# Scaled weight tables from PSUM, earlier weight loads, and a prologue divided otherwise between three engines

## Chip, cores and metric

One core of a Trainium2 chip. The metric is the device time of one execution in microseconds; a kernel is given by the median of several executions. Besides the time there is a traced execution of each kernel, whose span is about 1.8 us shorter than its time.

## The reference

```python
X = np.fft.fft(x, axis=1)               # x: 8 x 3008 x 256
X = np.fft.fft(X, axis=2).real          # mixing along sequence and model dimension
t = X.reshape(24064, 256)
out = (np.maximum(t @ w_gate, 0) * (t @ w_val)) @ w_out     # 256 -> 1536 -> 256
```

The kernel folds the second transform into the weights. `wc` and `ws` are cosine and sine transforms of `w_gate` and `w_val`, and `wm = s2 * ws` serves the mirrored half of the spectrum. The first transform is made in pieces of 94 x 32 points, with tables that the prologue makes from iotas and sines.

Of the kernel before, what the change touches and what calls it, by code (L numbers as in the profile page):

```python
# [11 lines left out]
F32 = mybir.dt.float32  # L12
BF16 = mybir.dt.bfloat16
I32 = mybir.dt.int32
ALU = mybir.AluOpType
ACTF = mybir.ActivationFunctionType
SB = bass.MemoryType.SB
PS = bass.MemoryType.PSUM
RND = 12582912.0
WARM = 15  # L20
FIRST = 15


# [21 lines left out]
def kernel(ctx: ExitStack, tc, x, w_gate, w_val, w_out, out):  # L45
# [3 lines left out]
    nc = tc.nc  # L49
    B, S, D = x.shape  # L50
    DF = w_gate.shape[1]
    NA, NB = 94, 32
# [100 lines left out]
    t1t = {}  # L153
# [27 lines left out]
    psf, tabs = {}, {}  # L181

    def ends(r, n):

        v = xt[0]["lo" if r < NB // 2 else "hi"][0:NA, r % 16:r % 16 + n, :]
        if r < NB // 2:
            nc.vector.tensor_copy(tabs["back"][:, r:r + n, 0:1], v[:, :, H:H + 1])
        else:
            nc.vector.tensor_copy(tabs["back"][:, r:r + n, 0:1], v[:, :, 0:1])
            nc.vector.tensor_copy(v[:, :, 0:1], v[:, :, H:H + 1])  # L190

    def back(r, n, evac):

        dst = tabs["back"][:, r:r + n, 1:H]
        src = free(xt[0]["lo" if r < NB // 2 else "hi"][0:NA], r % 16 * D + D - 1, [D, n], [-1, H - 1])
        if evac == "act":
            nc.scalar.copy(dst, src)
        else:
            nc.vector.tensor_copy(dst, src)
# [23 lines left out]
    def first_evac(c, evac):  # L223

        if 0 not in t1t:
            t1t[0] = tp.tile([128, 16, D], BF16, tag="t1", bufs=1, name="t1")
        dst = free(t1t[0][:], 2 * c, [1536, 2], [16, 96], [1, 2])
        src = free(psf[c], 0, [96, 2], [1, 96], [192, 2])
        plain = nc.scalar.copy if evac == "act" else nc.vector.tensor_copy
        plain(dst, src)  # L230
        if c == 0:
            plain(free(t1t[0][0:1], 1536, [16, 96]), psf[0][0:1, 384:480])
# [54 lines left out]
    w1 = const.tile([NA, 16, 96], BF16, tag="w1")  # L287
    wz = const.tile([NA, 3, 2, 96], BF16, tag="wz")
# [28 lines left out]
    def pair_w(n, i, eng, parts=(0, 1)):  # L317

        lo, hi, up = (wst[i, n, c] for c in range(3))
        if 0 in parts:  # L320
            eng.tensor_tensor(up, lo, hi, op=ALU.add)
        if 1 in parts:
            eng.tensor_tensor(lo, lo, hi, op=ALU.subtract)

    def fold_w(n, i, cs, ps=None):

        ps = ps or spare("psw")
        for k, w in ((0, wst[i, n, 2]), (1, wst[i, n, 0])):
            nc.tensor.matmul(ps[64 * k:64 * k + 64, :], lhsT=cd[:, cs, 64 * k:64 * k + 64], rhs=w,  # L329
                             start=True, stop=True)  # L330
        nc.scalar.copy((wc, ws)[cs][i][:, n * 512:(n + 1) * 512], ps[:])

    def scale_w(n, i):

        sl_ = slice(n * 512, (n + 1) * 512)
        nc.vector.tensor_scalar(wm[i][:, sl_], ws[i][:, sl_], scalar1=s2[:], scalar2=None, op0=ALU.mult)  # L336

    def nyquist():

# [6 lines left out]
    with tc.tile_pool(name="sp", bufs=1, space=SB) as sp:  # L346
        dve, pl = nc.vector, nc.gpsimd
# [14 lines left out]
        def absolute(out, a):  # L362
            nc.scalar.activation(out, a, ACTF.Abs)

        def iota(eng, out, pattern, base, mult):
            eng.iota(out, pattern=pattern, base=base, channel_multiplier=mult, allow_small_or_imprecise_dtypes=True)
# [26 lines left out]
        def warm(n):  # L393

            for k in range(n):
                nc.tensor.matmul(psk[:], lhsT=wk[:, 512:640], rhs=wk[:, 0:512], start=True, stop=True)
# [19 lines left out]
        iota(pl, kbi[:, 0, :], [[1, NB]], NB // 2, 0)  # L416
        iota(pl, kbi[:, 1:4, :], [[0, 3], [1, NB]], 0, 0)
        load_w(0, pl)
        iota(pl, di[:], [[-32, 4], [-16, 2], [-1, 16]], 0, 1)
        pl.memset(ro[:], 0.0)  # L420
        pl.tensor_scalar(s2[:], mi[:], scalar1=1.0, scalar2=-2.0, op0=ALU.min, op1=ALU.mult)

        def angles(lo, hi):
            t, q = tt[:, lo:hi, :], tq[:, lo:hi, :]
# [6 lines left out]
            cosines(free(wn[:], 1536 + 96 * a, [96, b_ - a], [2, 48]), tq[:, a:b_, :], S)  # L431
            sines(free(wn[:], 1536 + 96 * a + 1, [96, b_ - a], [2, 48]), tt[:, a:b_, :], S, -1.0)

        def negate(a, b_):
            dve.tensor_scalar(wn[:, 0, a:b_, :], wn[:, 1, a:b_, :], scalar1=-1.0, scalar2=None, op0=ALU.mult)  # L435

        def bits(shift, mask):
            ti = sp.tile([128, 1], I32, tag=f"b{shift}{mask}i")
            dve.tensor_scalar(ti[:], pi[:], scalar1=shift, scalar2=mask,
                              op0=ALU.logical_shift_right, op1=ALU.bitwise_and)  # L440
            tf = sp.tile([128, 1], F32, tag=f"b{shift}{mask}f")
            dve.tensor_copy(tf[:], ti[:])
            return tf

        def col(tag, a, *args, **kw):
            t = sp.tile([128, 1], F32, tag=tag)
            dve.tensor_scalar(t[:], a[:], *args, **kw)
            return t

        def group(cs, upper):  # L450
            for k in (0, 1):
                for c in cs:
                    first_products(c, upper, k)
# [3 lines left out]
        angles(9, J)  # L457
        dve.memset(wz[:], 0.0)
        table(9, 16)
        negate(1, 9)  # L460
        ends(0, 8)
        back(2, 6, "dve")
        group((1, 2, 3), False)
        warm(9)
        jj, sl, up, odd = bits(0, 15), bits(4, 1), bits(5, 3), bits(0, 1)
        z = col("z", jj, scalar1=0.0, scalar2=None, op0=ALU.is_equal)
        negate(9, 16)
        back(0, 2, "dve")
        both = (free(tt[:], 0, [16 * 48, 2], [1, 48]), free(tq[:], 0, [16 * 48, 2], [1, 48]))
        cosines(free(wz[:], 0, [97, 2], [2, 48]), both[1], S)  # L470
        for k in range(2):
            sines(free(wz[:], 192 * (k + 1), [97, 2], [2, 48]), both[0], S, 2.0 * k - 1.0)
        dve.tensor_scalar(tabs["wzn"][:], wz[:, 0], scalar1=-1.0, scalar2=None, op0=ALU.mult)
        nz = col("nz", z, scalar1=-1.0, scalar2=1.0, op0=ALU.mult, op1=ALU.add)
        mul = col("mul", z, scalar1=sl[:], scalar2=16.0, op0=ALU.mult, op1=ALU.mult)
        mul = col("mul2", mul, scalar1=jj[:], scalar2=None, op0=ALU.add)
        o0 = col("o0", nz, scalar1=sl[:], scalar2=-8.0, op0=ALU.mult, op1=ALU.mult)
        o0 = col("o1", o0, scalar1=8.0, scalar2=None, op0=ALU.add)
        o1 = col("o2", nz, scalar1=8.0, scalar2=o0[:], op0=ALU.mult, op1=ALU.add)
        nc.scalar.copy(w1[:, 1:16, :], wn[:, 1, 1:16, :])  # L480
        ends(24, 8)
        back(25, 3, "act")
        back(28, 3, "dve")
        back(24, 1, "act")
        back(31, 1, "dve")
        group((1, 2, 3), True)
        warm(2)
        ends(8, 4)
        dve.tensor_scalar(dd[:], dd[:], scalar1=mi[:], scalar2=None, op0=ALU.mult)
        residue(dd[:], dq[:], D, dve)  # L490
        back(8, 4, "act")
        first_evac(1, "dve")
        absolute(dq[:], dd[:])
        first_evac(2, "act")
        first_evac(3, "dve")
        cosines(cd[:, 0, 1:H], dq[:, 1:H], D)
        sines(cd[:, 1, 1:H], dd[:, 1:H], D, 1.0)
        dve.tensor_copy(cd[:, 1, 0:1], odd[:])
        dve.tensor_scalar(cd[:, 0, 0:1], odd[:], scalar1=-1.0, scalar2=1.0, op0=ALU.mult, op1=ALU.add)

        sv, ti = [], []

        def turns(cs):
            ti.append(sp.tile([128, 4, NB], I32, tag=f"m2i{cs}", name="ti"))
            sv.append(sp.tile([128, 4, NB], F32, tag=f"m2s{cs}", name="sv"))
            dve.tensor_scalar(ti[cs][:], kbi[:], scalar1=mul[:], scalar2=(o0, o1)[cs][:], op0=ALU.mult, op1=ALU.add)
            dve.tensor_scalar(ti[cs][:], ti[cs][:], scalar1=NB - 1, scalar2=None, op0=ALU.bitwise_and)
            nc.scalar.activation(sv[cs][:], ti[cs][:], ACTF.Sin, scale=2.0 * math.pi / NB * (1.0 - 2e-7), bias=npi[:])

        group((4, 5), False)  # L510
        warm(4)
        ends(20, 4)
        back(20, 4, "dve")
        group((4, 5), True)
        warm(2)
        ends(12, 4)
        ends(16, 4)
        back(12, 4, "act")
        back(16, 4, "act")
        turns(0)  # L520
        turns(1)
        dve.tensor_scalar(ui[:], ui[:], scalar1=up[:], scalar2=-1.0, op0=ALU.is_equal, op1=ALU.mult)
        first_evac(4, "act")
        first_evac(5, "dve")
        for cs in range(2):
            dve.tensor_tensor(m2[:, cs, :].rearrange("p (u k) -> p u k", u=4), sv[cs][:], ui[:], op=ALU.mult)
        group((6, 7, 0), False)
        warm(1)
        group((6, 7, 0), True)
        pair_w(0, 0, dve)  # L530
        first_evac(6, "act")
        nc.sync.dma_start(out=seen[:], in_=t1t[0][0:1, 0, 12:14])
        load_w(1, nc.sync)
        load_w(2, nc.sync)
        load_x(1, 0, nc.sync, False)
        first_evac(7, "dve")
        first_evac(0, "act")

        pl.tensor_scalar(ro[:, :, 0, 1:16], di[:, :, 0, 1:16], scalar1=16.0, scalar2=-1.0,
                         op0=ALU.is_equal, op1=ALU.mult)  # L540
        pl.tensor_scalar(ro[:, :, 1, 1:16], di[:, :, 1, 1:16], scalar1=-16.0, scalar2=None, op0=ALU.is_equal)
# [14 lines left out]
        stage2(0, 0, 0, "act")  # L556
        fold_w(0, 1, 0, g_tile())
        stage2(0, 0, 1, "dve")
        scale_w(0, 0)
        fold_w(0, 1, 1)  # L560
        scale_w(0, 1)

        pair_w(1, 0, pl)
        load_x(1, 0, None)
# [181 lines left out]
    def at(t, fn, *args):  # L746
        extra.setdefault(t, []).append(lambda: fn(*args))

    for n in (1, 2):
        for k, t in enumerate(((1, 2, 2, 3), (4, 5, 6, 7))[n - 1]):  # L750
            at(t, fold_w, n, k // 2, k % 2)
            if k % 2:
                at(t, scale_w, n, k // 2)
    for t, blk, cs, e in ((1, 1, 1, "dve"), (3, 1, 0, "dve"), (4, 2, 1, "dve"), (6, 2, 0, "dve")):
        at(t, upright, blk, cs, e)
    at(3, rotate, 0, 4, 8)
# [109 lines left out]
```

## The kernel before: what the change touches

Weights come in six 512-column parts (n = 0 to 2, i = 0 for gate, 1 for value). GpSimd or DVE make sums and differences (`pair_w`), TensorE folds them, ACT evacuates, and DVE scales the sine table, here from SBUF:

```python
    def fold_w(n, i, cs, ps=None):
        ps = ps or spare("psw")          # spare: one of two PSUM banks, by turns
        ...                              # two matmuls
        nc.scalar.copy((wc, ws)[cs][i][:, n * 512:(n + 1) * 512], ps[:])

    def scale_w(n, i):
        sl_ = slice(n * 512, (n + 1) * 512)
        nc.vector.tensor_scalar(wm[i][:, sl_], ws[i][:, sl_], scalar1=s2[:], scalar2=None, op0=ALU.mult)
```

Near the end of the prologue (cut):

```python
        group((4, 5), True)              # first products 4 and 5, upper half
        warm(2)                          # warm-up matmuls
        ...
        turns(0); turns(1)               # index (DVE), mask (DVE), sine (ACT)
        ...
        first_evac(4, "act")             # behind the two sines on ACT
        first_evac(5, "dve")
        ...
        group((6, 7, 0), False); warm(1); group((6, 7, 0), True)
        pair_w(0, 0, dve)
        first_evac(6, "act")
        nc.sync.dma_start(out=seen[:], in_=t1t[0][0:1, 0, 12:14])   # holds SP until evacuation 6
        load_w(1, nc.sync); load_w(2, nc.sync); load_x(1, 0, nc.sync, False)
        first_evac(7, "dve"); first_evac(0, "act")
```

Behind it comes a ramp of twelve steps into which the other folds are mixed; `rotate` is one small matmul with a small evacuation (a copy out of PSUM), and takes its bank (one PSUM buffer) from the same two as the folds. In the profiles `psw` are the products of the folds, `ps` the first products and stage 2's, `psr` that of a rotation; `G` and `V` are the gate and value products of a step, `h` their elementwise product, `po` the output products, and a product is called mirrored when its table is `wm`:

```python
    for n in (1, 2):
        for k, t in enumerate(((1, 2, 2, 3), (4, 5, 6, 7))[n - 1]):
            at(t, fold_w, n, k // 2, k % 2)
            if k % 2:
                at(t, scale_w, n, k // 2)
    ...
    at(3, rotate, 0, 4, 8)
    at(6, rotate, 0, 8, NKA)
```

## Time and profile before

| | kernel before |
|---|---|
| time, median of 3 | 629.81 us (629.6 to 630.03) |
| span traced | 628.5 us (an execution of 630.34 us) |
| first product of the weight tables (`psw`) | 18.68 us |
| first output product (`po`) | 55.25 us |
| 289th output product (the first of the second batch) | 130.38 us |

I read every trace by these marks, in us from the start of the span. Up to the first `psw` lies the prologue; from there to the first `po` the ramp; up to the 289th `po` the end of the first batch and the entry of the second. (The recorded expectations count the products from 0 and call the 289th the 288th.) What a kernel gains is read between marks, not from the busy shares.

The other view is the list of TensorE's waits (engine, line, tile, releaser: us in total, times, longest), between 20 and 56 us:

```profile
PE V L638 <- DVE h L651: 1.5, 3, 0.7
PE psr L259 <- ACT wc L331: 0.4, 1, 0.4
PE psr L259 <- ACT ws L331: 0.4, 1, 0.4
PE G L630 <- ACT gs L625: 0.2, 1, 0.2
```

So the ramp holds 2.5 us of waits: 1.5 for products `h` (the longest, 0.7, behind the two held tables of the first step), 0.8 for two rotations (`psr`), which wait for the evacuation of the fold whose bank they take. The same view from 56 to 620 us has two lines:

```profile
PE V L638 <- DVE E L645: 0.8, 1, 0.8
PE psr L259 <- ACT gs L625: 0.2, 1, 0.2
```

Both lie between the first and the 289th output product. The scaling's mean, over all six, hides 0.35 us (at 35.06, beside no arithmetic of GpSimd's) and 1.08 (at 46.54, beside an operation of GpSimd's) (group: count, then busy us and mean ns):

```profile
L336 DVE TENSOR_SCALAR wm<-ws,s 128x512 bf16<-128x512 bf16 x6 | 5.3, 887 | 2.8 <-ACT ws L331 2.8
```

### The profile page before, as it was taken

What the parts mean: (1) busy time and instruction counts of PE and PEld (TensorE: products, weight loads), DVE (VectorE), ACT (ScalarE), POOL (GpSimd) and SP (SyncE); (2) the same over time, 40 slices, a digit from 0 to 9 for tenths busy, and PEclk for the clock granted to TensorE, in tenths of its full rate; (3) what the DMA queues carried; (4) which work ended last, traced back from release to release, by engine and by line L of the source; (5) the groups of instructions that cost most, each with busy time, mean ns of one, the idle gap of its engine ahead of it and who ended that gap; (6) DMA issues with size and microseconds to landing.
All of it is one profiled execution on the core that took longest, in us unless ns stands there. A gap on an engine that the chain in (4) does not pass through costs nothing.

```text
span 628.5 us, 11983 instructions
## 1 busy us (share of the span) xinstructions
PE 616.9 (98%) x4292; PEld 410.0 (65%) x4292; DVE 541.4 (86%) x660; ACT 444.0 (71%) x851; POOL 518.1 (82%) x445
## 2 busy tenths in 40 slices
PE   8999999999999999999999999999999999999996
PEld 4335666666666666666666666766666666666665
DVE  8677997999988998899988988899988889899991
ACT  7567777777777777777777777777687777766661
POOL 7677998998989988988989989899988866565665
PEclk9999999999999999999999999999999999999999
DMA  7697156613734263722826147441732124212114
GB/s 167 188 182 145 32 151 163 151 33 109 199 93 101 62 194 83 170 51 76 205 69 148 34 136 172 106 109 41 211 81 68 33 84 116 60 33 67 33 35 98
DMA packets 42597, 67.44 MB, mean 107 GB/s; under 512 B 5872, under 2 KB 32521, under 8 KB 40521
## 3 DMA queue, kind: packets, MB, share of 16 engines
q1 hardware_dynamic: 37944, 51.38, 32.8%
q0 software_dynamic: 4432, 15.11, 10.1%
q8 instruction: 33, 0.54, 0.4%
q14 instruction: 28, 0.22, 0.1%
q10 hardware_dynamic: 160, 0.20, 0.1%
HBM read 38.85 MB, written 30.17 MB: 110 GB/s over the span
## 4 chain that ended last, share of the span: by engine, by line
PE 94%; DVE 3%; issue 1%; ACT 1%; POOL 0%; POOLq 0%; DVEq 0%
PE po L687 40%; PE V L638 20%; PE G L630 10%; PE G L624 10%; PE G L623 9%; PE ps L162 2%; PE psw L329 2%; PE ps L271 2%; DVE h L651 1%; PE ps L216 0%; PE ps L166 0%; DVE wm L336 0%; DVE wn L435 0%; DVE E L645 0%; PE pst L240 0%
## 5 line engine op out<-in xcount | busy, mean ns | idle before, releaser
L658 POOL TENSOR_TENSOR h<-gm,E 128x992 bf16<-128x992 f32 (+1 forms) x138 | 319.9, 2318 | 83.3 <-DVE E L665 53.5
L687 PE MATMUL po<-wo,h 128*128 128x256 bf16 (+2 forms) x2304 | 328.7, 273 | 0.0
L687 PEld LDWEIGHTS <-h 128*128 128x128 bf16 (+2 forms) x2304 | 231.2, 103 | 106.0
L632 ACT ACTIVATE gm<-G 128x496 f32<-128x496 f32 (+1 forms) x288 | 170.4, 592 | 95.6 <-PE G L630 88.3
L651 DVE TENSOR_TENSOR h<-gs,V 128x1024 bf16<-128x1024 f32 (+3 forms) x150 | 173.7, 1158 | 59.8 <-PE V L638 43.2
L645 DVE SCALAR_TENSOR_TENSOR E<-nb,af,V 128x496 f32<-128x496 bf16 (+1 forms) x276 | 190.1, 730 | 1.8 <-PE G L624 1.8
L625 ACT ACTIVATE gs<-G 128x497 f32<-128x497 f32 (+2 forms) x288 | 169.6, 589 | 25.0 <-PE G L624 24.8
L665 DVE SCALAR_TENSOR_TENSOR E<-E,V 128x992 f32<-128x992 f32 (+1 forms) x138 | 164.3, 1190 | 0.0
L630 PE MATMUL G<-pq,wm 128*128 128x496 bf16 (+1 forms) x288 | 108.0, 375 | 0.3 <-ACT gs L625 0.2
L624 PE MATMUL G<-pq,ws 128*128 128x497 bf16 (+2 forms) x288 | 108.0, 375 | 0.0
L623 PE MATMUL G<-pq,wc 128*128 128x497 bf16 (+2 forms) x288 | 108.0, 375 | 0.0
L638 PE MATMUL V<-pq,ws 128*128 128x497 bf16 (+2 forms) x288 | 85.4, 375 | 0.8 <-DVE E L645 0.8
L638 PE MATMUL V<-pq,wc 128*128 128x497 bf16 (+2 forms) x288 | 85.5, 375 | 0.0
L624 PEld LDWEIGHTS <-ws 128*128 128x128 bf16 x288 | 28.2, 98 | 32.7
L700 ACT COPY os<-po 128x512 f32<-128x512 f32 x63 | 36.9, 586 | 14.7 <-PE po L687 13.8
L638 PEld LDWEIGHTS <-wc 128*128 128x128 bf16 x288 | 28.1, 98 | 20.8 <-issue 2.7
L114 POOL TENSOR_TENSOR eo<-xla 94x256 bf16<-94x256 f32 x56 | 40.3, 729 | 0.8
L623 PEld LDWEIGHTS <-wc 128*128 128x128 bf16 x288 | 28.1, 98 | 18.5 <-issue 1.2
L114 POOL TENSOR_TENSOR eo<-xlb 94x256 bf16<-94x256 f32 (+1 forms) x42 | 34.4, 820 | 0.9
L111 POOL TENSOR_TENSOR xla<-xla,xha 94x510 f32<-94x510 f32 x28 | 32.9, 1175 | 2.2
L177 ACT CAST t<-ps 96x512 bf16<-96x512 f32 x56 | 32.7, 583 | 2.4 <-PE ps L162 0.2
L630 PEld LDWEIGHTS <-wm 128*128 128x128 bf16 x288 | 28.1, 98 | 5.2 <-issue 2.6
(141 smaller groups left out, 373.9 us busy)
## 6 DMA issues: line engine op xcount, KB each, us to landing
out_dram<-os SPq DMA_DIRECT2D x124, 128.0 KB
Td<-t SPq DMA_DIRECT2D x7, 768.0 KB
t<-Td SPq DMA_DIRECT2D x7, 768.0 KB
out_dram<-os SPq DMA_DIRECT2D x82, 64.0 KB
xla<-in_x_dram SPq DMA_DIRECT2D x7, 720.0 KB
xlb<-in_x_dram SPq DMA_DIRECT2D x7, 640.0 KB
nb<-Nd SPq DMA_DIRECT2D x23, 128.0 KB
out_dram<-os SPq DMA_DIRECT2D x40, 48.0 KB
```

The costliest lines, as they stand in the source:

```text
L114: yield eng.tensor_tensor(e1[:, :, k:k + H], x1[:, :, 0:H], free(x1, D, [DX, n], [-1, H]), op=op)
L623: nc.tensor.matmul(G[:, ds], lhsT=wc[0][:, fs], rhs=pq[:, 0, ds], start=True, stop=False)
L624: nc.tensor.matmul(G[:, ds], lhsT=ws[0][:, fs], rhs=pq[:, 1, ds], start=False, stop=True)
L625: nc.scalar.activation(pair(t, "gs")[:, t % 2, ds], G[:, ds], ACTF.Relu)
L630: nc.tensor.matmul(G[:, cols], lhsT=wm[0][:, f * 128:(f + 1) * 128], rhs=pqt[b, blk][:, 1, cols], start=False, stop=True, skip_group_check ...
L632: nc.scalar.activation(pair(t, "gm")[:, t % 2, cols], G[:, cols], ACTF.Relu)
L638: nc.tensor.matmul(pair(t, "V")[:, t % 2, cs], lhsT=w[:, f * 128:(f + 1) * 128], rhs=pqt[b, blk][:, min(k, 1), cs], start=(k == 0), stop=( ...
L645: nc.vector.scalar_tensor_tensor(pair(t, "E")[:, t % 2, cols], nbt[b, blk][:, cols], af[:, f:f + 1], pair(t, "V")[:, t % 2, cols], op0=ALU ...
L651: nc.vector.tensor_tensor(pair(t, "h")[:, k, 0, 0:ds.stop - ds.start], pair(t, "gs")[:, k, ds], pair(t, "V")[:, k, ds], op=ALU.mult)
L658: eng.tensor_tensor(free(pair(t, "h")[:], 1024 * (t % 2) + 512 + w - 1, [1024, n], [-1, w]), pair(t, "gm")[:, k, cols], val[:, k, cols], o ...
L665: nc.vector.scalar_tensor_tensor(E[:, :, cols], E[:, :, cols], 2.0, V[:, :, cols], op0=ALU.mult, op1=ALU.subtract)
L687: nc.tensor.matmul(po[0:m, i, :], lhsT=pair(t - f + ff, "h")[:, ff % 2, sg, g * 128:g * 128 + m], rhs=wo[:, ff, :], start=(ff == 0), stop= ...
```

## The change

Its intent: read the scaling's input from PSUM, so that GpSimd no longer holds the scaling up (1.08 us against 0.35 in the trace of before); let W1 and W2 load earlier; release products 6, 7 and 0 earlier by evacuating product 4 ahead of the sines; and give DVE less to do in the prologue. Evacuations 5 and 7 go from DVE to ACT and evacuation 0 from ACT to DVE. The core of the diff (the other moved lines of the prologue cut):

```diff
-WARM = 15
+WARM = 12
@@ fold_w
-        nc.scalar.copy((wc, ws)[cs][i][:, n * 512:(n + 1) * 512], ps[:])
-    def scale_w(n, i):
-        nc.vector.tensor_scalar(wm[i][:, sl_], ws[i][:, sl_], scalar1=s2[:], ...)
+        nc.scalar.copy((wc, ws)[cs][i][:, sl_], ps[:])
+        if cs:
+            nc.vector.tensor_scalar(wm[i][:, sl_], ps[:], scalar1=s2[:], ...)
@@ prologue: turn indices on GpSimd, masking of both at once on DVE
+            pl.tensor_scalar(ti[cs], kbi[:], scalar1=mul[:], scalar2=(o0, o1)[cs][:], ...)
+        dve.tensor_scalar(tis[:], tis[:], scalar1=NB - 1, scalar2=None, op0=ALU.bitwise_and)
-        negate(9, 16)                                            # DVE
+        nc.scalar.mul(wn[:, 0, 9:16, :], wn[:, 1, 9:16, :], -1.0)   # ACT
@@ after the upper halves of groups (1,2,3), (4,5), and inside (6,7,0)
-        warm(2)
-        warm(2)
-        warm(1)
@@ order on ACT
-        turns(0)
-        turns(1)
         first_evac(4, "act")
-        nc.sync.dma_start(out=seen[:], in_=t1t[0][0:1, 0, 12:14])
+        nc.sync.dma_start(out=seen[:], in_=t1t[0][0:1, 0, 8:10])
         load_w(1, nc.sync)
         load_w(2, nc.sync)
         ...
+        for cs in range(2):
+            nc.scalar.activation(sv[cs][:], ti[cs], ACTF.Sin, ...)
```

More of the change, by code (lines that the diff above doesn't have):

```diff
@@ L330, in fold_w @@
                              start=True, stop=True)
-        nc.scalar.copy((wc, ws)[cs][i][:, n * 512:(n + 1) * 512], ps[:])
-    def scale_w(n, i):
         sl_ = slice(n * 512, (n + 1) * 512)
-        nc.vector.tensor_scalar(wm[i][:, sl_], ws[i][:, sl_], scalar1=s2[:], scalar2=None, op0=ALU.mult)
+        nc.scalar.copy((wc, ws)[cs][i][:, sl_], ps[:])
+        if cs:
+            nc.vector.tensor_scalar(wm[i][:, sl_], ps[:], scalar1=s2[:], scalar2=None, op0=ALU.mult)
     def nyquist():
@@ L418 @@
         load_w(0, pl)
-        iota(pl, di[:], [[-32, 4], [-16, 2], [-1, 16]], 0, 1)
-        pl.memset(ro[:], 0.0)
-        pl.tensor_scalar(s2[:], mi[:], scalar1=1.0, scalar2=-2.0, op0=ALU.min, op1=ALU.mult)
         def angles(lo, hi):
@@ L432, in table @@
             sines(free(wn[:], 1536 + 96 * a + 1, [96, b_ - a], [2, 48]), tt[:, a:b_, :], S, -1.0)
-        def negate(a, b_):
-            dve.tensor_scalar(wn[:, 0, a:b_, :], wn[:, 1, a:b_, :], scalar1=-1.0, scalar2=None, op0=ALU.mult)
         def bits(shift, mask):
@@ L459 @@
         table(9, 16)
-        negate(1, 9)
+        dve.tensor_scalar(wn[:, 0, 1:9, :], wn[:, 1, 1:9, :], scalar1=-1.0, scalar2=None, op0=ALU.mult)
         ends(0, 8)
@@ L464 @@
         warm(9)
-        jj, sl, up, odd = bits(0, 15), bits(4, 1), bits(5, 3), bits(0, 1)
-        z = col("z", jj, scalar1=0.0, scalar2=None, op0=ALU.is_equal)
-        negate(9, 16)
-        back(0, 2, "dve")
         both = (free(tt[:], 0, [16 * 48, 2], [1, 48]), free(tq[:], 0, [16 * 48, 2], [1, 48]))
@@ L472 @@
             sines(free(wz[:], 192 * (k + 1), [97, 2], [2, 48]), both[0], S, 2.0 * k - 1.0)
-        dve.tensor_scalar(tabs["wzn"][:], wz[:, 0], scalar1=-1.0, scalar2=None, op0=ALU.mult)
+        nc.scalar.mul(wn[:, 0, 9:16, :], wn[:, 1, 9:16, :], -1.0)
+        nc.scalar.copy(w1[:, 1:10, :], wn[:, 1, 1:10, :])
+        back(0, 2, "dve")
+        jj, sl, up, odd = bits(0, 15), bits(4, 1), bits(5, 3), bits(0, 1)
+        z = col("z", jj, scalar1=0.0, scalar2=None, op0=ALU.is_equal)
         nz = col("nz", z, scalar1=-1.0, scalar2=1.0, op0=ALU.mult, op1=ALU.add)
@@ L479 @@
         o1 = col("o2", nz, scalar1=8.0, scalar2=o0[:], op0=ALU.mult, op1=ALU.add)
-        nc.scalar.copy(w1[:, 1:16, :], wn[:, 1, 1:16, :])
+        dve.tensor_copy(cd[:, 1, 0:1], odd[:])
+        dve.tensor_scalar(cd[:, 0, 0:1], odd[:], scalar1=-1.0, scalar2=1.0, op0=ALU.mult, op1=ALU.add)
+        sv, ti = [], []
+        tis = sp.tile([128, 2, 4, NB], I32, tag="m2i")
+        for cs in range(2):
+            ti.append(tis[:, cs])
+            sv.append(sp.tile([128, 4, NB], F32, tag=f"m2s{cs}", name="sv"))
+            pl.tensor_scalar(ti[cs], kbi[:], scalar1=mul[:], scalar2=(o0, o1)[cs][:], op0=ALU.mult, op1=ALU.add)
+        pl.tensor_scalar(ui[:], ui[:], scalar1=up[:], scalar2=-1.0, op0=ALU.is_equal, op1=ALU.mult)
         ends(24, 8)
@@ L486 @@
         group((1, 2, 3), True)
-        warm(2)
         ends(8, 4)
+        back(8, 4, "act")
         dve.tensor_scalar(dd[:], dd[:], scalar1=mi[:], scalar2=None, op0=ALU.mult)
         residue(dd[:], dq[:], D, dve)
-        back(8, 4, "act")
+        first_evac(2, "act")
         first_evac(1, "dve")
+        first_evac(3, "dve")
+        dve.tensor_scalar(tis[:], tis[:], scalar1=NB - 1, scalar2=None, op0=ALU.bitwise_and)
         absolute(dq[:], dd[:])
-        first_evac(2, "act")
-        first_evac(3, "dve")
         cosines(cd[:, 0, 1:H], dq[:, 1:H], D)
         sines(cd[:, 1, 1:H], dd[:, 1:H], D, 1.0)
-        dve.tensor_copy(cd[:, 1, 0:1], odd[:])
-        dve.tensor_scalar(cd[:, 0, 0:1], odd[:], scalar1=-1.0, scalar2=1.0, op0=ALU.mult, op1=ALU.add)
-        sv, ti = [], []
-        def turns(cs):
-            ti.append(sp.tile([128, 4, NB], I32, tag=f"m2i{cs}", name="ti"))
-            sv.append(sp.tile([128, 4, NB], F32, tag=f"m2s{cs}", name="sv"))
-            dve.tensor_scalar(ti[cs][:], kbi[:], scalar1=mul[:], scalar2=(o0, o1)[cs][:], op0=ALU.mult, op1=ALU.add)
-            dve.tensor_scalar(ti[cs][:], ti[cs][:], scalar1=NB - 1, scalar2=None, op0=ALU.bitwise_and)
-            nc.scalar.activation(sv[cs][:], ti[cs][:], ACTF.Sin, scale=2.0 * math.pi / NB * (1.0 - 2e-7), bias=npi[:])
+        dve.tensor_scalar(tabs["wzn"][:], wz[:, 0], scalar1=-1.0, scalar2=None, op0=ALU.mult)
         group((4, 5), False)
@@ L514 @@
         group((4, 5), True)
-        warm(2)
         ends(12, 4)
+        back(12, 4, "act")
         ends(16, 4)
-        back(12, 4, "act")
-        back(16, 4, "act")
-        turns(0)
-        turns(1)
-        dve.tensor_scalar(ui[:], ui[:], scalar1=up[:], scalar2=-1.0, op0=ALU.is_equal, op1=ALU.mult)
-        first_evac(4, "act")
-        first_evac(5, "dve")
-        for cs in range(2):
-            dve.tensor_tensor(m2[:, cs, :].rearrange("p (u k) -> p u k", u=4), sv[cs][:], ui[:], op=ALU.mult)
-        group((6, 7, 0), False)
-        warm(1)
-        group((6, 7, 0), True)
-        pair_w(0, 0, dve)
-        first_evac(6, "act")
-        nc.sync.dma_start(out=seen[:], in_=t1t[0][0:1, 0, 12:14])
+        back(16, 4, "dve")
+        group((6, 7, 0), False)
+        first_evac(4, "act")
+        nc.sync.dma_start(out=seen[:], in_=t1t[0][0:1, 0, 8:10])
         load_w(1, nc.sync)
@@ L535 @@
         load_x(1, 0, nc.sync, False)
-        first_evac(7, "dve")
-        first_evac(0, "act")
+        first_evac(5, "act")
+        pair_w(0, 0, dve)
+        for cs in range(2):
+            nc.scalar.activation(sv[cs][:], ti[cs], ACTF.Sin, scale=2.0 * math.pi / NB * (1.0 - 2e-7), bias=npi[:])
+        group((6, 7, 0), True)
+        first_evac(6, "act")
+        first_evac(7, "act")
+        first_evac(0, "dve")
+        for cs in range(2):
+            dve.tensor_tensor(m2[:, cs, :].rearrange("p (u k) -> p u k", u=4), sv[cs][:], ui[:], op=ALU.mult)
+        nc.scalar.copy(w1[:, 10:16, :], wn[:, 1, 10:16, :])
+        iota(pl, di[:], [[-32, 4], [-16, 2], [-1, 16]], 0, 1)
+        pl.tensor_scalar(s2[:], mi[:], scalar1=1.0, scalar2=-2.0, op0=ALU.min, op1=ALU.mult)
         pl.tensor_scalar(ro[:, :, 0, 1:16], di[:, :, 0, 1:16], scalar1=16.0, scalar2=-1.0,
@@ L558 @@
         stage2(0, 0, 1, "dve")
-        scale_w(0, 0)
         fold_w(0, 1, 1)
-        scale_w(0, 1)
         pair_w(1, 0, pl)
@@ L751 @@
             at(t, fold_w, n, k // 2, k % 2)
-            if k % 2:
-                at(t, scale_w, n, k // 2)
     for t, blk, cs, e in ((1, 1, 1, "dve"), (3, 1, 0, "dve"), (4, 2, 1, "dve"), (6, 2, 0, "dve")):
```

## The prediction

> **What bounds the kernel now.** I read the page first (busy shares and slices), then the chain of waits in its first 60 us, then the timeline of that stretch, then, for the changed kernel, the compiled order of instructions with their semaphores.
>
> ```profile
> PE 616.9 (98%) x4292; PEld 410.0 (65%) x4292; DVE 541.4 (86%) x660; ACT 444.0 (71%) x851; POOL 518.1 (82%) x445
> PE   8999999999999999999999999999999999999996
> ```
>
> Only PE is full in every slice. By stretches it is busy 100.0 us of each 100 from 200 to 600 us, and the diff touches no line of that stretch. What the change is worth must come from the prologue (to 24 us) and the ramp (24 to 55 us, twelve steps t = 0 to 11 into which the folds of the weights are mixed). If PE enters the steady part earlier by x, the end moves by x. The chain of waits (start, us, what) shows where PE is held there:
>
> ```profile
> 14.92 0.40 ACT sv L508
> 15.32 0.40 ACT t L230
> 15.76 0.24 PE ps L216
> ...
> 23.70 1.50 DVE wm L336 x2
> 25.19 0.87 issue
> 26.06 0.67 DVE h L651
> ...
> 34.44 0.59 ACT ws L331
> 35.08 0.17 PE psr L259
> ...
> 47.54 0.66 DVE h L658
> 48.20 0.59 DVE h L651
> ```
>
> From 0.9 to 14.9 us the chain is DVE's. Between these places it is matmuls back to back. The four holds: first products 6, 7 and 0 wait for the evacuation of product 4, which stands behind two sines on ACT; the first h waits for two scaled tables; a rotation waits for the evacuation that frees its PSUM buffer; the h of step 8 waits behind a scaled table. Why these tables are slow is in the timeline:
>
> ```profile
> 23.37 1.27 POOL L321 TENSOR_TENSOR wst<-wst 128x512 f32<-128x512 f32 x1 [4.02 <-DMA wst<-in_moe_w_gate_dram]
> 23.70 2.43 DVE L336 TENSOR_SCALAR wm<-ws,s 128x512 bf16<-128x512 bf16 x2
> 24.72 1.26 POOL L323 TENSOR_TENSOR wst<-wst 128x512 f32<-128x512 f32 x1
> 35.06 0.35 DVE L336 TENSOR_SCALAR wm<-ws,s 128x512 bf16<-128x512 bf16 x1 [0.60 <-ACT ws L331]
> 46.30 1.18 POOL L111 TENSOR_TENSOR xla<-xla,xha 94x510 f32<-94x510 f32 x1
> 46.54 1.08 DVE L336 TENSOR_SCALAR wm<-ws,s 128x512 bf16<-128x512 bf16 x1 [0.73 <-ACT ws L331]
> ```
>
> Alone the scaling takes 0.35 us; beside a POOL operation it ends about 0.14 us after that one does (46.30 + 1.18 + 0.14 = 47.62, and 24.72 + 1.26 + 0.15 = 26.13).
>
> [...] I take 0.69 us from this trace's evacuation of the same shape (DVE L246 pst, 128x512, mean 688 ns). [...] the new scaling waits for ACT's semaphore, not PE's, so it still starts only after ACT's copy of the same bank. [...] Dropping warm-up matmuls leaves gaps below 1 us, so I count nothing; the trace of before shows gaps up to 0.41 us without a slowdown.
>
> **The change part by part.** Times below are on the clock of the old trace, and where they lie in the changed kernel they are estimates from its durations.
>
> (a) First products 1 to 3. Three of 15 warm-ups at 0.43 us go, but the last three were partly fast: products start at about 6.55 instead of 7.11. This gains nothing, since the upper half waits for the first high load, which ACT saw land at 9.41. On DVE, the second negation (0.68 of chain) goes to ACT, where 0.75 us lie beside idle time; the wzn table (0.13) goes later, two one-column copies (0.15) come in front. DVE is then free by about 9.2 and waits for the load; its two column moves take 0.65, so the upper half starts at 10.1, not 10.48: 0.37 gained, and two warm-ups (0.43) less before products 4 and 5.
>
> (b) The new hold. The turn indices are now made on POOL, after its four weight loads, the last of which ends at 10.70 + 1.07 = 11.77. POOL took 0.71 us for a 128x128 tensor-scalar and 0.45 to 0.50 for 128x60, so two take until about 13.2. The masking of both stands on DVE ahead of the moves of high load 20 to 23. DVE, ready at 12.45, stands still until 13.3, and then possibly until POOL's next operation lets go (13.95). With masking 0.3, wzn 0.13 and moves 0.35, products 4 and 5 upper can go at 14.1 to 14.7; before, 13.76. So most of (a) is lost.
>
> (c) Products 6, 7, 0. Product 4 is complete at about 14.7 to 15.2, ACT evacuates it at once (0.49; the sines come later), and product 0 starts at 15.25 to 15.75, not 15.76. From there to the end of the group is 18.75 - 15.76 = 2.99, less one warm-up (0.22): it ends at 18.0 to 18.5, not 18.75. Gain 0.2 to 0.7, say 0.5.
>
> (d) First step. After the group PE has fold, uprights, fold: 1.01 + 0.58 + 1.01 = 2.60. ACT copies ws (0.66 with its delay), then DVE scales wm for 0.69, and now this stands ahead of the small evacuation of the rotation (0.17). That is done 4.2 after the group, the fold of W1 part already 4.0 after: stage 2 loses 0.27. The second table: fold ends 5.6 after the group, copy 6.25, scaling 6.3 to 7.0, h 7.0 to 7.65, mirrored V 7.7. Before it came 26.77 - 18.75 = 8.02 after. Net gain 0.3.
>
> (e) Step 3. The rotation's PSUM buffer is that of the fold before it, and now two readers hold it: the copy until 35.03, then the scaling until 35.03 + 0.03 + 0.69 = 35.75. PE starts the rotation at 35.80 instead of 35.08: 0.72 lost on the path.
>
> (f) Step 7. The scaling takes 0.69 for 1.08, and DVE is the chain from there to 54 us (each V waits for the h before it), so 0.35 gained. The other three scalings lie beside matmuls.
>
> (g) W1 and W2 are released by evacuation 4, at about 15.3, not by evacuation 6 near 18.7: the loads come some 3.4 us earlier. POOL's 4.02 us wait for them shrinks, but the fold at 27.56 had its input at 25.98, so PE gains nothing. POOL also gets its memset back (0.24), and its sums end near 19.3 as before.
>
> Sum: 0.5 + 0.3 - 0.72 + 0.35 = 0.43 us gained; with a little for a steadier POOL I say 0.5: 629.8 - 0.5 = 629.3.
>
> **Rivals.** First: the hold of (b) does not appear, because POOL is quicker with the indices than the row of perm says. Then product 0 can start at 14.7, the group ends at 17.5, and (c) is worth 1.2: 628.5. For it speaks that perm's 0.71 lay beside DVE work; against it that the loads' issue alone lasts to 11.77. Second: the hold is longer, each DVE operation being shut out by POOL's string of small ones (tables, then the rotation matrix, up to 16.7), so that the last DVE moves and the first pair of W0 come late: nothing is gained in the prologue, (e) remains, 630.2. Third: the early W loads meet the rest of the first loads on the DMA engines, busy 1.00 between 7 and 15 us; but the release is at 15.3, when those have landed (0.04 from 15 to 20). I give this little; it would cost a few tenths. Fourth: the gain of the ramp is taken back in the steady part, by a late load or POOL; there PE waits for neither, and POOL comes in earlier, so no.
>
> **Range and chances.** The uncertain terms are (c) by 0.4, (d) and (f) by 0.2 each, (e) by 0.15, and the runs themselves by 0.2 (629.6 to 630.03): together about 0.6, hence 628.4 to 630.0. Two per cent is 12.6 us, more than the whole stretch touched could give without PE's own work there vanishing: faster 0.01, same 0.985, slower 0.005.
>
> **What would show it.** The end of the first products at 18.0 to 18.5; DVE standing before the masking of the turn indices, released by POOL; all six scalings near 0.69 us whether POOL works or not; the rotation of step 3 released by DVE, 0.7 us later against its fold; the first pair of W1 on POOL near 20 instead of 23.4; the steady part shifted as a block. I am wrong if the group ends by 17.5 or after 18.8, if the scalings are still held by POOL, if step 3 shows no hold, or if the shift at 55 us is not that of the end.

The 0.69 us are taken for scaling, from another operation of DVE; that it would not be held, and that gaps of TensorE below 1 us cost no clock, were no more than my estimates when this was written.

## The result, and the profile after

The changed kernel took 628.73 us (628.66 to 630.43, 4 runs) beside 629.92 (629.6 to 630.09, 4 runs) of the kernel before. A ratio here is the mean time of one kernel's fast runs over that of the other's of the same rounds, so it is not quite the ratio of the medians: 0.9988, 95% interval 0.9971 to 1.0005. That is the same time at two per cent, and the interval includes no gain at all.

| mark, us | before | after | gained up to there | gained in the stretch |
|---|---|---|---|---|
| first `psw` | 18.68 | 17.52 | 1.16 | 1.16 |
| first `po` | 55.25 | 54.28 | 0.97 | -0.19 |
| 289th `po` | 130.38 | 128.68 | 1.70 | 0.73 |
| end | 628.54 | 626.94 | 1.60 | -0.10 |

The medians differ by 1.19 us only; the traced execution of the kernel before, at 630.34 us, was slower than any of its four timed ones.

TensorE's share did not move. The weight loads (PEld) are 4284, eight fewer than before: the eight warm-ups that were dropped. That the matmuls are 40 fewer is in part a matter of records: the same kernel has 4284 in c0's trace, so 32 are missing here:

```profile
PE 613.0 (98%) x4252; PEld 408.9 (65%) x4284; DVE 538.8 (86%) x656; ACT 444.2 (71%) x852; POOL 520.0 (83%) x447
```

**Prologue.** In the chain of waits (start, us, what) the two sines are gone from ACT's place ahead of evacuation 4, which starts 1.06 us earlier (15.32 before):

```profile
13.66 0.58 PE ps L216 x6
14.24 0.02 issue
14.26 0.51 ACT t L230
...
14.82 0.24 PE ps L216
```

The hold that the prediction expected before the masking of the turn indices is there, but small. GpSimd's two index operations (timeline: start, us, engine, line) took 0.87 us together, and DVE stood 0.19 us for them:

```profile
11.84 0.87 POOL L481 TENSOR_SCALAR tis<-kbi,t 128x128 int32<-128x128 f32 x2
```

```profile
12.74 0.29 DVE L497 TENSOR_SCALAR tis<-tis 128x256 int32<-128x256 int32 x1 [0.19 <-POOL tis L481]
```

**Ramp.** All six scalings are now alike, 751 ns:

```profile
L334 DVE TENSOR_SCALAR wm<-psw,s 128x512 bf16<-128x512 f32 x6 | 4.5, 751 | 4.8 <-ACT ws L332 3.8 <-issue 0.9
```

But TensorE's waits between 20 and 56 us are not fewer. They have changed their names:

```profile
PE psr L259 <- DVE wm L334: 1.1, 1, 1.1
PE V L629 <- DVE h L642: 0.5, 1, 0.5
PE psr L259 <- ACT wc L332: 0.4, 1, 0.4
PE ps L271 <- DVE t L260: 0.3, 1, 0.3
PE G L621 <- ACT gs L616: 0.3, 1, 0.3
```

The waits for `h` fell from 1.5 to 0.5 us. The rotation of step 3 waits 1.1 us instead of 0.4, since its bank is now read twice, by ACT's copy and then by the scaling; and stage 2 waits 0.3 us for the small evacuation behind the scaling. The sum is 2.6 us, where it was 2.5.

**Second batch's entry.** From 56 to 620 us one line is left:

```profile
PE V L629 <- DVE E L636: 0.3, 1, 0.3
```

against 0.8 and 0.2 before. The change touches nothing there. Whether this is of the change or of the run was the first question for the experiments.

### The profile page after: what moved, and what is told of

It reads as the page before. It is cut to its first block, busy times and chain, and to the rows that moved or that the text cites. A ratio compares the mean times of both kernels' runs of the same rounds, so it can differ in the third digit from the quotient of the medians.

```text
span 626.9 us, 11935 instructions
## 1 busy us (share of the span) xinstructions
PE 613.0 (98%) x4252; PEld 408.9 (65%) x4284; DVE 538.8 (86%) x656; ACT 444.2 (71%) x852; POOL 520.0 (83%) x447
## 4 chain that ended last, share of the span: by engine, by line
PE 93%; DMA 3%; DVE 1%; issue 1%; ACT 1%; POOL 1%; POOLq 0%; DVEq 0%; ACTq 0%
PE po L678 39%; PE V L629 18%; PE G L614 10%; PE G L621 9%; PE G L615 9%; PE ps L162 2%; PE psw L329 2%; PE ps L271 2%; DMA lo<-in_x_dram 1%; DMA Td<-t 1%; DMA t<-Td 1%; PE ps L216 1%; DVE h L642 0%; ACT ws L332 0%; PE ps L166 0%
## 5 line engine op out<-in xcount | busy, mean ns | idle before, releaser
L629 PE MATMUL V<-pq,ws 128*128 128x512 bf16 (+2 forms) x279 | 83.5, 374 | 0.3 <-DVE E L636 0.3
L629 PE MATMUL V<-pq,wc 128*128 128x496 bf16 (+2 forms) x266 | 80.7, 374 | 0.0
```

The costliest lines, as they stand in the source:

```text
L629: nc.tensor.matmul(pair(t, "V")[:, t % 2, cs], lhsT=w[:, f * 128:(f + 1) * 128], rhs=pqt[b, blk][:, min(k, 1), cs], start=(k == 0), stop=( ...
```

## The experiments

Twelve runs, all correct; c0 is the changed kernel itself. The table gives the marks of every traced run; "wait" is the sum of TensorE's waits between the first and the 289th `po`, and the last column is that stretch less the wait.

| run | first `psw` | `psw` to first `po` | to 289th `po` | wait | rest | median time | ratio to before (95%) |
|---|---|---|---|---|---|---|---|
| before | 18.68 | 36.57 | 75.13 | 1.06 | 74.07 | 629.92 | |
| changed | 17.52 | 36.76 | 74.40 | 0.27 | 74.13 | 628.73 | 0.9988 (0.9971-1.0005) |
| c0 | 17.43 | 36.77 | 75.24 | 1.08 | 74.16 | 629.35 | 0.9989 (0.9971-1.0008) |
| a1 | 19.31 | 36.71 | 74.77 | 0.60 | 74.17 | 630.37 | 1.0002 (0.9983-1.0021) |
| a2 | 18.47 | 35.47 | 74.42 | 0.2 | 74.2 | 628.80 | 0.9984 (0.9964-1.0005) |
| a3 | 17.86 | 36.79 | 74.39 | 0.3 | 74.1 | 629.34 | 0.9990 (0.9972-1.0009) |
| b1 | 17.73 | 35.96 | 74.90 | 1.0 | 73.9 | 629.44 | 1.0007 (0.9985-1.0030) |
| b3 | 17.42 | 34.97 | 75.22 | 1.15 | 74.07 | 627.65 | 0.9973 (0.9955-0.9992) |
| b6 | 17.43 | 36.77 | 73.96 | 0 | 73.96 | 628.59 | 0.9991 (0.9975-1.0008) |
| w | 17.82 | 36.77 | 74.35 | 0.5 | 73.9 | 629.20 | 0.9996 (0.9979-1.0013) |
| l | 17.44 | 36.77 | 74.86 | 0.79 | 74.07 | 629.05 | 0.9990 (0.9973-1.0007) |
| d1 | 17.42 | 34.97 | 74.06 | 0.15 | 73.91 | 628.45 | 0.9978 (0.9963-0.9993) |
| d2 | 17.42 | 38.04 | 73.92 | 0 | 73.92 | 627.88 | 0.9987 (0.9948-1.0026) |
| d3 | 17.36 | 34.96 | 74.72 | 0.82 | 73.90 | 627.60 | 0.9975 (0.9955-0.9995) |

The times alone can't carry a theory of tenths: one kernel's executions can lie 2 to 3 us apart, in d2 6. The marks can, because a kernel repeats them (c0 against the changed kernel: 17.43 and 17.52, 36.77 and 36.76), except where a DMA decides. A trace is still one execution.

### c0: the changed kernel again

No edit.

> The changed kernel once more, to see how firm its 1.2 us are and how often the 630.4 us of one run in four comes. Both theories: about 628.7 us, 1.2 below the kernel before; PE enters the first output products at 54.3 us (before: 55.25). If the gain after 55 us (0.65 us, which I put down to the row broadcast of batch 1 landing in time) is chance, it will differ between runs of one kernel: hold of E near 105 us anywhere from 0 to 0.9 us.

Measured: 629.35 us (629.22 to 629.58) beside 629.99. The expected time, about 628.7, was missed. Prologue and ramp came out as in the first trace of the changed kernel; the stretch to the 289th `po` did not, and TensorE's waits from 56 to 620 us say why:

```profile
PE V L629 <- DVE E L636: 1.1, 1, 1.1
```

The same kernel waited 1.1 us here and 0.3 there. So the 0.73 us that the first trace gained in that stretch are not the change's. The table makes it general: the stretch took 73.92 to 75.24 us, but less its waits always 73.9 to 74.2.

### a1: only the scaling from PSUM

```diff
 # in the kernel before: fold_w as in the change, all scale_w calls removed
```

> The kernel before with the scaling from PSUM alone. My theory: first step 0.25 us earlier, step 3 about 0.75 us later (the rotation waits for the second reader of its bank), step 7 about 0.3 us earlier: first output products at 55.3 to 55.6 us (before 55.25), time 0 to 0.4 us above before. Rival (the stated intent): freeing the scaling from POOL is where the gain comes from, then it is 0.5 to 1.2 us below before.

Measured: 36.71 us from `psw` to `po`, 0.14 more than before. By its parts: 0.33 gained in the first step, 0.77 lost at the rotation of step 3, 0.33 gained at the scaling of step 8's table. The absolute marks are later because the first high load landed late in this run (ACT's first reversed rows start at 10.03, in the other traces of the kernel before and its variants at 8.80 to 9.41). The PSUM scaling alone is worth nothing, as expected.

### a2: only the early loads

```diff
-        nc.sync.dma_start(out=seen[:], in_=t1t[0][0:1, 0, 12:14])
+        nc.sync.dma_start(out=seen[:], in_=t1t[0][0:1, 0, 8:10])
```

> The kernel before with the loads of W1 and W2 behind evacuation 4 alone. My theory: POOL's first pair of W1 starts 3 us earlier, PE nothing: first output products at 55.25 within 0.15 us, time within 0.2 us of before, unless the row broadcast near 105 us moves. Rival: the early loads shift POOL and the later transfers, and with them the 0.6 us found after 55 us: time 0.5 us below before with the hold near 105 us shorter.

This missed. The ramp took 35.47 us, 1.10 less than before and 1.29 less than the changed kernel. GpSimd's pair operations on W1 (timeline) came at 21.59 instead of 23.37, were done by 24.21, and the two scalings that had taken 2.43 us took 0.86 and 0.35:

```profile
21.59 1.27 POOL L321 TENSOR_TENSOR wst<-wst 128x512 f32<-128x512 f32 x1 [2.45 <-DMA wst<-in_moe_w_gate_dram]
```

```profile
23.49 0.86 DVE L336 TENSOR_SCALAR wm<-ws,s 128x512 bf16<-128x512 bf16 x1
24.52 0.35 DVE L336 TENSOR_SCALAR wm<-ws,s 128x512 bf16<-128x512 bf16 x1 [0.16 <-ACT ws L331]
```

So the loads do not gain by giving the fold its input earlier, as I had thought of them, but by moving GpSimd out of the scalings' way: 0.75 us of the 1.10 lie in the first step, 0.35 at the scaling of step 8's table. How firm this is, one trace can't tell. The first mirrored value matmul came 7.34 us after the first `psw` here, but 7.90 in b1 and 9.41 in d2, which also read SBUF after early loads; and the interval of the times includes no gain.

### a3: only evacuation 4 ahead of the sines

```diff
+        first_evac(4, "act")
         turns(0)
         turns(1)
-        first_evac(4, "act")
 # the two products m2 on DVE go behind first_evac(7)
```

> The kernel before with evacuation 4 ahead of the two sines on ACT (and the two products for m2 behind evacuation 7, so that DVE is not held instead). My theory: product 0 starts at 15.2 instead of 15.76, the fold after the first products at 18.2 instead of 18.7, first output products at 54.7: about half of the 1.16 us that the whole change gained there. Rival: the lighter DVE earned it, and the order on ACT is worth under 0.15 us.

Measured: first `psw` at 17.86, 0.82 earlier. Part of that need not be the order on ACT: the reversed rows of the first high load start at 8.80 here and at 9.41 in the trace of before. a2 has the prologue of before and its rows at 8.83, and its first `psw` came at 18.47; beside it a3 gains 0.61, about what was expected. The chain of waits (10 to 19 us) is then TensorE alone, and warm-up matmuls (L396) are in it:

```profile
14.33 0.43 PE psk L396 x2
...
16.24 0.22 PE psk L396
```

What is left to gain in the prologue is thus what these cost. The ramp keeps its held scalings (36.79).

### w: the warm-ups back in the changed kernel

```diff
-WARM = 12
+WARM = 15
+        warm(2)    # and warm(2), warm(1) at their old places
```

> The changed kernel with all warm-up matmuls back (15 at the start, 2, 2 and 1 between the groups). My theory: the last one is 0.22 us on the path and the pair ahead of products 6 and 7 about 0.2, the others fill idle time: the fold after the first products at 17.8 to 18.1 us (changed kernel 17.4 to 17.5). Rival: they keep the clock up or cost nothing: 17.5 or less.

Measured: first `psw` at 17.82, 0.30 to 0.39 later, as expected, and the ramp unchanged (36.77). Of the rival's clock the other traces show that TensorE's was granted at 1.00 from 7 to 20 us with these warm-ups (before) and without them (the changed kernel). Compared where the first high load landed alike, a3 gains 0.61 on a2 (rows at 8.80 and 8.83) and w loses 0.39 on c0 (9.09 and 8.97): 1.00 us together, where c0 is 1.04 ahead of a2. By this sum the regrouping of the small work on DVE, ACT and GpSimd is worth about nothing; it was not run alone.

### b1: the changed kernel with the scaling from SBUF

```diff
-        if cs:
-            nc.vector.tensor_scalar(wm[i][:, sl_], ps[:], ...)
+    def scale_w(n, i): ...                 # and its six calls, as before
```

> The changed kernel with the scaling put back to the bf16 copy in SBUF. My theory now (after the loads alone gained as much as the PSUM scaling was to gain): the early loads have moved POOL's sums off the scalings, so PSUM is no longer needed for that, and its price, the rotation of step 3 held by a second reader, goes: rotation released by ACT again, first output products 0.5 to 1.0 us earlier than in the changed kernel (53.3 to 53.8 us against 54.2 to 54.3). Rival: the scalings meet POOL elsewhere (steps 2 and 7) and the gain is eaten: 54.2 to 54.8.

Measured: the ramp took 35.96 us, 0.81 less than the changed kernel, within what was expected, with scalings of 0.34, 1.16, 0.81, 0.35, 0.35 and 0.47 us. With early loads, SBUF was the better source in this execution. Its times don't confirm it: 628.61, 631.35, 630.19 and 628.69. The traced one is the fastest of them. What the slow ones did was not traced; the slowest has a mean granted clock of 0.995, the others 0.997 or 0.998, and d2's trace below has a stretch at a granted clock of 0.51.

### l: the changed kernel with late loads

```diff
 # seen, load_w(1), load_w(2), load_x(1, 0) back behind first_evac(6), seen reading 12:14
```

> The changed kernel with the loads of W1 and W2 put back behind evacuation 6. My theory: the early loads help only scalings that read SBUF, since they move GpSimd's pair operations out of the scalings' way, and a scaling that reads PSUM takes 0.75 us whether GpSimd works or not. So nothing moves: the first output product at 54.1 to 54.35 us (changed kernel 54.20 and 54.28), counted from the first product of the tables 36.7 to 36.85 us (36.77 and 36.76). Rival: the loads are worth 0.75 us here too, as they were alone (first output product 54.9 to 55.1, 37.5 from the tables).

Measured: first `psw` 17.44, ramp 36.77: no change. GpSimd's pair operations came late and lay beside a scaling, which took its 0.75 us all the same:

```profile
22.70 1.26 POOL L321 TENSOR_TENSOR wst<-wst 128x512 f32<-128x512 f32 x1 [3.31 <-DMA wst<-in_moe_w_gate_dram]
24.05 1.27 POOL L323 TENSOR_TENSOR wst<-wst 128x512 f32<-128x512 f32 x1
```

```profile
23.86 0.75 DVE L334 TENSOR_SCALAR wm<-psw,s 128x512 bf16<-128x512 f32 x1 [0.94 <-ACT ws L332]
```

So the two parts of the change buy the same thing. In their traces the loads alone gained 1.10 us of the ramp, PSUM alone -0.14, both together -0.19.

### b3: the rotations first in steps 3 and 7

```diff
+    at(3, rotate, 0, 4, 8)
+    at(7, rotate, 0, 8, NKA)
     for n in (1, 2):
         for k, t in enumerate(...):        # folds
     ...
-    at(3, rotate, 0, 4, 8)
-    at(6, rotate, 0, 8, NKA)
```

> The changed kernel with the two early rotations put ahead of the folds (step 3: before that step's fold; the second in step 7 instead of 6), so that neither waits for a buffer that was filled just before. My theory: the idle 1.14 us of PE in step 3 and 0.35 us in step 6 go, and nothing takes their place: first output products at 52.7 to 53.0 us. Rival: DVE or the loads of W2 bind in steps 4 to 7, then under 0.7 us comes through: after 53.6.

If the price of PSUM is the bank that the rotation waits for, a rotation that takes the bank ahead of the fold does not pay it. Measured: first `po` at 52.39, the ramp 1.80 us shorter than in the changed kernel, and both waits for `psr` are gone from TensorE's list (20 to 56 us):

```profile
PE V L629 <- DVE h L642: 0.5, 1, 0.5
PE G L621 <- ACT gs L616: 0.3, 1, 0.3
```

More came than expected: 1.32 us between the second and fourth mirrored value matmul, so also the part of the wait that step 3 had before the change, and 0.49 up to the eighth, where the second rotation had waited 0.4 us for `wc`. 627.65 us (627.12 to 629.04), 0.9973 with an interval below one.

### b6: the load of the second batch's x two steps later

```diff
-enumerate((5, 24) if b else (14, 31))
+enumerate((5, 24) if b else (14, 33))
```

> The changed kernel with the second load of batch 2 issued in step 33 instead of 31, behind the one-row write of batch 1 instead of just ahead of it. My theory: that write (1 KB) took 5.2 to 6.1 us to land because it queued behind the load; now it lands in under 3 us, E near 105 us waits no more, and from the first to the 288th output product it takes 74.1 us or less (74.40 and 75.24 in the two runs of the changed kernel, 75.13 before). Time 0.3 to 1.0 us below the changed kernel, and firmer. Rival: the write is slow by itself or the wait moves to the folds of batch 2: no change.

`E` needs a row that goes to HBM (1 KB, `Nd`) and comes back to all partitions (`nb`), issued by SP. In c0 the write was issued at 96.86 and the read, which waits for it, at 103.00: 6.1 us, behind a load of x (SP's timeline):

```profile
96.86 0.24 SPq L282 DMA_DIRECT2D Nd<-pq  x1
103.00 0.35 SPq L283 DMA_DIRECT2D nb<-Nd  x1
```

In b6, with the load behind it:

```profile
96.83 0.23 SPq L282 DMA_DIRECT2D Nd<-pq  x1
97.93 0.34 SPq L283 DMA_DIRECT2D nb<-Nd  x1
```

1.1 us, TensorE waits for nothing, and the stretch takes 73.96 us, the least up to then. The write of the next row, now behind the load, took 5.7 us, and TensorE did not wait for it. The median of 628.59 is 0.14 and 0.76 us below those of the changed kernel, where 0.3 to 1.0 was expected. The load has a part that SP issues and one that GpSimd issues. In the trace of the changed kernel both were issued ahead of the write (GpSimd's at 92.42, landing 7.0 us after its issue, SP's from 93.16, the write at 96.91), and the write took 5.3 us. With SP's part behind it the write took 1.1 us in b6, d1 and d2, but 3.1 in d3. What held it in d3, and whether GpSimd's part was under way there, was not shown; nor how the 6.1 us of c0 divide between the two parts. The other wait, for the transpose through HBM (`t<-Td`), stays a matter of the run: 0.15 us in d1 and 0.82 in d3. (The 0.2 us of `psr` in before, a2 and b3 end with an evacuation by ACT instead.)

### d1: rotations first and x later

The edits of b3 and b6 together.

> The changed kernel with the rotations first in steps 3 and 7 and the load of the second batch's x two steps later: the two gains should add, since one lies before the first output product and the other behind it. First output product 52.3 to 52.5 us, 73.9 to 74.2 us from there to the 288th, median 626.6 to 627.3 us. Rival: the end takes back what the beginning gives (a time of 627.6 as with the rotations alone).

Measured in the trace: first `po` at 52.39, 74.06 from there, end at 624.53, 4.00 us before that of the kernel before: the gains add in this execution. It was the fastest of five, though (626.34; the others 627.13 to 628.82), and the median of 628.45 missed what I expected and is not better than b3's.

### d2: d1 with the scaling from SBUF

The edits of d1 and b1 together.

> As d1, with the scalings read from SBUF again. With the rotation no longer behind the scaling, PSUM costs only 0.75 us against 0.35 to 0.69 in four scalings that the tensor engine may or may not wait for, and spares ACT and GpSimd nothing. I expect it within 0.3 us of d1 at the first output product, either way. If a PSUM scaling is the better choice only because it doesn't meet GpSimd, d2 should show scalings over 0.8 us and be later than d1.

(No trace shows 0.69 us for a scaling from SBUF; b1's four shorter ones took 0.34 to 0.47.)

The trace shows the case against SBUF. The two first scalings took 2.11 and 1.41 us (DVE's timeline; the line covers both):

```profile
22.75 3.44 DVE L336 TENSOR_SCALAR wm<-ws,s 128x512 bf16<-128x512 bf16 x2
```

The first began at 22.75, while GpSimd issued an indirect load (22.33 to 23.38) and 0.66 us before its pair operation, and ended at 24.86, 0.17 us after the pair operation that came next (23.41 to 24.69). The second began at 24.78 and ended 0.15 us after the pair operation behind that (24.77 to 26.04). In b1 the first, beside the same issue, took only 0.34 (in a2 the second 0.35), and b1's second took 1.16. When a scaling beside such an issue is held was not shown. TensorE stood 0.73 us at 24.2 and 1.11 us at 25.7. Then something came that no trace before had shown. The table by stretches (columns: us, busy us and count of each engine, granted clock of TensorE, DMA share, GB/s) has, for d2 and then for d1:

```profile
24.00:27.20 3.20, 1.35 (x6) 0.50 (x6) 2.78 (x4) 1.44 (x3) 3.12 (x3) 1.00 1.13 209
27.20:30.60 3.40, 3.40 (x13) 0.96 (x11) 1.59 (x3) 0.59 (x1) 3.24 (x4) 0.51 1.16 231
```

```profile
27.20:30.60 3.40, 3.40 (x18) 1.09 (x16) 2.25 (x4) 2.09 (x5) 3.24 (x4) 1.00 1.18 241
```

TensorE was busy for 1.35 us of 3.2, and its granted clock was 0.51 in the next 3.4 us and 0.99 in the 3.4 behind those. That the one brought the other is my reading of one trace. The hold cost 1.6 us up to the first mirrored value matmul (26.83 against 25.24 in d1), and the clock 1.6 us more up to the second (4.17 us between them against 2.60). All thirteen other traces have a granted clock of 1.00 in that stretch; the next least busy, the kernel before and a3, had TensorE busy for 2.35 and 2.34 of the 3.2 us, stood at most 0.69 us at once, and kept their clock. The changed kernel stood 1.14 us at once at 33.3, busy for 2.68 of the 3.4 us from 30.6, and had 1.00 there and from 34 to 37 us too.

The times again do not follow the one trace: five of six executions took 627.12 to 629.38 and one 633.41. So d2 is not shown slower than d1; shown is that a scaling from SBUF can be caught like this, and one from PSUM was in none of nine traces. The lowest mean clocks are not SBUF's alone: 0.994 in d2's slowest execution, but also in d3's (629.82), and 0.995 in d1's (628.82), which both read PSUM; these were not traced.

### d3: d1 with evacuations 1 and 3 earlier on DVE

```diff
+        first_evac(1, "dve")
         ends(8, 4)
         back(8, 4, "act")
+        first_evac(3, "dve")
         dve.tensor_scalar(dd[:], dd[:], scalar1=mi[:], ...)
         residue(dd[:], dq[:], D, dve)
 # both removed from their old places; the masking of tis goes behind back(16, 4)
```

> As d1, with evacuations 1 and 3 ahead of DVE's small work on the frequency angles, and the masking of the turns behind the last reversed rows. In the changed kernel the tensor engine stood 1.01 us at 12.14 us for evacuation 1. If that wait is on the path to the tables, the first product of the tables comes 0.4 to 0.9 us earlier (16.6 to 17.1 us instead of 17.4 to 17.5) and so does the first output product (51.5 to 52.1 us). Rival: the wait is hidden anyway, since the last rows land and are reversed late, and the tables' start stays within 0.2 us.

The rival held. TensorE's wait for evacuation 1 shrank from 1.01 us in the changed kernel (0.96 in d1) to 0.15, and the tables began only 0.06 us earlier (17.36 against 17.42). The chain of waits shows what took its place: the angles now come later on DVE, their sines and the next reversed rows on ACT are late, and evacuation 4 stands behind them:

```profile
13.11 0.40 ACT cd L358
13.51 0.20 ACT cd L354
13.71 0.51 ACT back L197
14.21 0.41 ACT t L230
```

A wait of 1 us on the busiest engine was worth nothing, since another chain ended at the same moment. 627.6 us (626.57 to 629.82), interval below one, not to be told from b3 or d1.

## Why the prediction was right or wrong, point by point

The time was right: 629.3 predicted, 628.73 measured, and 629.35 when repeated. Its terms were not all right; two errors of the same direction, one of them a matter of chance, fell within the range. Two of its signs of being wrong came: the shift at 55 us was not that of the end, and the first products ended at its limit of 17.5 us (17.59 in the first trace, 17.50 in c0, before 18.75).

- **(a), (b), (c), prologue, +0.5: too small.** Measured +1.16, so the first rival came true (1.2). The mis-sized term is (b): I gave GpSimd 0.71 us for each index operation, after the row of the permutation table, and so a hold of some 0.85 us. Two took 0.87 us, 0.44 each (a third operation of 128 x 128, with other arithmetic, 0.85), and DVE stood 0.19; its masking then took 0.29 us beside that third operation (12.70 to 13.55), so it was not shut out as the second rival had it. The hold was thus put 0.66 us too long, as much as the gain was put too small. In c0 GpSimd's index operations lie on the chain, and the tables still began at 17.43. The gain itself is evacuation 4 ahead of the sines (a3: 0.61 to 0.82) and the warm-ups (w: 0.30 to 0.39).
- **(d), first step, +0.3: right.** The first mirrored value matmul came 8.09 us after the first `psw` before and 7.81 after: 0.28. Stage 2's wait of 0.3 us for the small evacuation came too.
- **(e), step 3, -0.72: right.** -0.78 between the second and fourth mirrored value matmul. b3 shows that the bank is the cause: take it earlier and the loss is gone.
- **(f), +0.35: right.** 2.39 us to 2.06 between the eighth and ninth. The scaling takes 751 ns, not the 690 that I took from a copy of the same shape.
- **(g), loads, 0: right here, by half a reason.** l confirms that they gain nothing in the changed kernel. My reason, that the fold had its input in time anyway, overlooked that a GpSimd operation costs also by when it runs (the first two scalings: 2.43 us in the trace of before, 0.86 and 0.35 in a2). Alone the loads gained most in a trace's ramp (a2: 1.10), once.
- **"The steady part shifted as a block", and the fourth rival's "PE waits for neither": wrong.** The shift was 0.97 us at 55 us and 1.60 at the end. The step that failed is the assumption that TensorE waits for nothing from 55 us on, so that nothing there depends on the run. Two waits do, nearly all of it for DMAs, 0 to 1.15 us in all; c0 lost in them what the first trace had gained. So, of the 1.6 us in the trace, 0.97 lie where the change acts: +1.16 in the prologue, and the ramp's 0.28 - 0.78 - 0.02 + 0.33 = -0.19.
- **Scalings near 0.69 and no longer held: right** in every trace with PSUM as the source: 0.75 us each, in l also beside a pair operation.
- **"Gaps below 1 us, so I count nothing" for the clock: right for this kernel**, though the prediction read the trace of before too low: 0.41 us is the largest gap between its first products, but in the ramp it has one of 0.68, also without a slowdown. The changed kernel itself stood 1.01 us at once in the prologue and 1.14 in the ramp, with a granted clock of 1.00 in both stretches. d2 stood 1.84 us in two pieces within 2.7 us, and there the clock was 0.51 afterwards.

Not settled: how often an execution falls into d2's case or b1's slow times, how little work of TensorE's brings a slow clock (1.35 us of 3.2 went before one in d2, 2.34 in a3 did not), and which of b3, d1 and d3 is the fastest. All three are 0.2 to 0.3% faster than the kernel before. Whether they are faster than the changed kernel rests on their marks (b3's ramp: 1.80 us less) and on medians of different calls; they were not timed against each other in one call.

## What to carry to other kernels

Here a second reader kept a PSUM bank longer (the rotation of step 3 waited 1.1 us instead of 0.4): before moving a read to PSUM, look at who takes that bank next, and put the small user in front. If two edits take the same engine out of the way of the same operation, test each alone; here their gains did not add (ramp: 1.10 us for the loads, -0.14 for PSUM, -0.19 for both), and the price of one may exceed what is left for it. Before explaining tenths at the end of a trace, trace the same kernel twice and take out the waits that DMAs decide (0 to 1.15 us here).
